# Activation halves one tile later, 64-bit conversion begun later, and tiles moved by 320 bytes in a one-core attention + MoE kernel

## The chip, the cores and the metric

The kernel runs on one core of one Trainium2 chip, as one launch. The metric is the device time of the launch in microseconds (us), the median of three runs. Engines are named as the profile names them: PE is TensorE, ACT is ScalarE, DVE is VectorE, POOL is GpSimd, SP issues DMAs. PEld is PE's weight load.

## The reference: what is computed

Three blocks follow one another.

1. Attention over q, k, v of 2 batches x 8 heads x 768 tokens x 64. Each row of q and k falls into one of 64 buckets by the signs of a projection; scores outside the own bucket are masked, then softmax and the product with v. The result, laid out as 1536 tokens x 512, is x.
2. A mixture of 4 experts, w1[e] 512 x 1024 and w2[e] 1024 x 512: the sum over e of p[:, e] * (relu(x @ w1[e]) @ w2[e]).
3. One dense layer pair on the result: h = x @ w_in (512 x 2048), g = 0 where h <= -1, h where h >= 1, (h + 1)^2 / 4 between, and the output is g @ w_out (2048 x 512). w_in and w_out arrive as 64-bit floats.

## The kernel before

**Units and jobs.** The hidden columns of blocks 2 and 3 are cut into 12 units u of 512: units 0 to 7 are the experts, 8 to 11 the dense pair. The tokens are cut into 12 tiles of 128. A *job* is one unit with a group of two or three token tiles; a job has four *tiles* f of 128 hidden columns. For each tile `l1b(j, f)` makes the first product on PE in a PSUM tile `mm` (12 matmuls of 384 columns, two buffers) and its activation on ACT, DVE and POOL; `l2b(j, f)` multiplies the activation of the job before with the second weight (9 matmuls of 512 columns into `o0`, `o1`, `o2`). Numbers are split into a high and a low half of 16 bits, so each activation leaves as `hh` and `hl`.

**First part (to about 445 us).** Attention and the first jobs, `JOBS_A`, are ordered together by the class `Order`, a list scheduler with costs and due times. The diff does not touch it.

**Second part, from the line `attx.close()`.** The order of the program is the order of the code. The main loop runs over jobs j and tiles f: `l1b(j + 1, f)`, a transposed token tile (`x_all`) if one is due, `step(j)`, `l2b(j, f)`, `step(j)`. Every engine executes its own instructions in this order. J0 is the first job of this part, JF = J0 + 2 the first with 16-bit weights. The units run 0, 2 to 6, 1 (two jobs each), then 7 and 8 to 11 (four jobs each).

**`step(j)`** fetches weights that are due (list `late`), moves one piece of x to 16 bits (`x_f16`, list `xq`, eight pieces), advances the bound of x for the dense pair (`x2_steps`), advances both weight generators (`w_steps`: the scan L1075 for the largest magnitude, `fin` for the scale, `conv_w` for the two 16-bit halves, L1194 to L1199) and advances `w64_steps` by one. `w64_steps` turns a 64-bit weight tile into f32: a load `r64`, one ACT instruction (`m64`, L1139), five on DVE (L1141 to L1150), and the scan on ACT (L1154 calls L1075); at most 16 finished tiles wait (`w64_ahead`).

**Riders.** `fin` needs a transpose and a small matmul on PE. They ride in the unused columns 384:512 of the next `mm` tile: `rider(ps)`, called right behind the tile's matmuls, issues the PE instruction and its small DVE instructions (`turn_over`, L1088 to L1095; `spread`, L1097 to L1101).

**The activation of units 8 to 11 (L1332 to L1337),** per tile: ACT reads `mm` twice (`ga`, `gg`), DVE squares `ga`, POOL adds it to `gg`, ACT scales the sum into `hh`, DVE makes `hl`:

```
act.activation(a[:, 0:n], ps[:, 0:n], AF.Relu, bias=half, scale=kh)
act.activation(gg[:, 0:n], ps[:, 0:n], AF.Relu, bias=nhalf, scale=kh)
dve.scalar_tensor_tensor(a[:, 0:n], a[:, 0:n], 1.0, a[:, 0:n], ALU.min, ALU.mult)
pool.tensor_tensor(gg[:, 0:n], gg[:, 0:n], a[:, 0:n], ALU.add)
act.activation(hh[:, 0:n], gg[:, 0:n], AF.Copy, scale=cc)
dve.scalar_tensor_tensor(hl[:, 0:n], gg[:, 0:n], cc, hh[:, 0:n], ALU.mult, ALU.subtract)
```

`mm` is free again when ACT has read it twice. `kh` and `cc` come from `k5` (`scales2`), made at a unit's first tile (for unit 8 at each job's first tile).

**Memory.** The tiles of pool `const` come first, then all others. `ident` is 512 bytes per partition, the others are small, rounded up to 32 bytes; they add up so that x0, acc, the weights and nearly all other large tiles begin 64 bytes past a multiple of 128 (192 past one of 256). The kv tiles xk0 to xk3, kb and vs are 3136, 3072 and 3072 bytes, 9280 together, so xk0 to xk3 stand at 192, 0, 64 and 128 past a multiple of 256.

Of the kernel before, what the change touches and what calls it, by code (L numbers as in the profile page):

```python
# [8 lines left out]
F32 = mybir.dt.float32  # L9
# [277 lines left out]
def attn_moe_kernel(ctx: ExitStack, tc, q, k, v, proj, probs, w1, w2, w_in, w_out, out):  # L287
# [668 lines left out]
    with tc.manual_schedule():  # L956
# [87 lines left out]
        r64 = ctx.enter_context(tc.tile_pool(name="r64", bufs=2))  # L1044
        s64 = ctx.enter_context(tc.tile_pool(name="s64", bufs=1))
        x16_p = ctx.enter_context(tc.tile_pool(name="x16", bufs=1))
        mode["h"] = h_p = ctx.enter_context(tc.tile_pool(name="hb", bufs=8))
        g_p = ctx.enter_context(tc.tile_pool(name="g", bufs=2))
        raw2_p = ctx.enter_context(tc.tile_pool(name="raw2", bufs=4))
        w64_ahead = 16  # L1050
        w64_p = ctx.enter_context(tc.tile_pool(name="w64", bufs=w64_ahead + 2))
# [3 lines left out]
        J0, J1 = len(JOBS_A), len(jobs)  # L1055
        JF = J0 + 2
        jobs_of = {u: [j for j, x in enumerate(jobs) if x[0] == u and j >= JF] for u in LB}
        late, pend, turn, x2q, xq = [], [], [], [], []
        seen, x_done = {1: set(), 2: set()}, []

        def mm_tile():
# [19 lines left out]
        def fin(am, n, e_out, s_out, age=2):  # L1081
            mx = t_p.tile([128, 1], F32, tag="mx", name="mx2")
            mt = t_p.tile([1, 1], F32, tag="mt", name="mt")
            dg = t_p.tile([1, 1], BF16, tag="dg", name="dg2")
            left = [2]
            dve.tensor_reduce(mx, am[:, 0:n], AX.X, ALU.max)

            def turn_over(ps):  # L1088
                pe.transpose(ps[0:1], mx, ident)
                dve.tensor_reduce(mt, ps[0:1], AX.X, ALU.max)  # L1090
                dve.tensor_scalar(mt, mt, 2.0 ** -100, 2.0 ** -14, ALU.max, ALU.mult)
                pow2(mt)
                dve.tensor_copy(dg, mt)
                left[0] -= 1
                soon(spread, age)  # L1095

            def spread(ps):  # L1097
                pe.matmul(ps[:, 0:1], ones[0:1], dg, start=True, stop=True)
                dve.tensor_copy(e_out, ps[:, 0:1])
                dve.reciprocal(s_out, ps[:, 0:1])  # L1100
                left[0] -= 1  # L1101

            soon(turn_over, age)
            while left[0]:
                yield "fin"
# [5 lines left out]
        def w64_steps():  # L1111
            order = []
            for u in range(8, 12):
                order += [(1, u, f) for f in range(4)] + [(2, u, f) for f in range(4)]
            rt = {}

            def fetch(i):
                if i >= len(order):
                    return
                kind, u, f = order[i]  # L1120
                s = 4 * u - 32 + f
                t = rt[i] = r64.tile([128, 512, 2], I32, tag="r64", name="r64")
                if kind == 1:
                    sp.dma_start(
                        t.rearrange("p (c f) t -> p c (f t)", c=KC),
                        w_in32[:, s * 256:s * 256 + 256].rearrange("(c p) f -> p c f", p=128),
                    )
                else:
                    sp.dma_start(t.rearrange("p f t -> p (f t)"), w_out32[s * 128:s * 128 + 128, :])

            for i in range(2):
                fetch(i)
            for i, key in enumerate(order):
                r = rt.pop(i)
# [12 lines left out]
                dve.scalar_tensor_tensor(m, r.bitcast(U16)[:, :, 1], 2.0 ** -36, m, ALU.mult, ALU.mult)  # L1147
                fetch(i + 2)
                yield
                dve.tensor_tensor(wv, t.bitcast(F32), m, ALU.add)  # L1150
                kind, u, f = key
                if f == 0:
                    am64[kind, u] = t_p.tile([128, 4], F32, tag="am64", name="am64", bufs=6)
                scan(wv, am64[kind, u][:, f:f + 1])  # L1154
                w64_t[key] = wv
                yield

        w64 = w64_steps()

# [43 lines left out]
        def w_steps(kind):  # L1203
            for n, u in enumerate(LB):
                if n == 0:
                    ew[kind, u], sw[kind, u] = ew_b[:, kind - 1:kind], sw_b[:, kind - 1:kind]
                else:
                    if u < 8:
                        am = t_p.tile([128, 4], F32, tag=f"am{kind}", name=f"am{kind}", bufs=2)
                        for f in range(4):  # L1210
                            while (kind, u, f) not in raw2:
                                yield False
                            scan(raw2[kind, u, f], am[:, f:f + 1])
                            yield
                    else:
                        while (kind, u, 3) not in w64_t:
                            yield "w64"
                        am = am64[kind, u]
                    ew[kind, u] = const.tile([128, 1], F32, name=f"ew{kind}_{u}")
                    sw[kind, u] = const.tile([128, 1], F32, name=f"sw{kind}_{u}")  # L1220
                    yield from fin(am, 4, ew[kind, u], sw[kind, u])
                for f in range(4):
                    while ((JF - 1 if n < 2 else jobs_of[LB[n - 2]][-1]), f) not in seen[kind]:
                        yield False
                    conv_w(kind, n, f)
                    yield

        wgen = {1: w_steps(1), 2: w_steps(2)}

        def need(kind, u, f):  # L1230
            while (kind, u, f) not in w16:
                got = next(wgen[kind])
                if got is False:
                    raise RuntimeError(f"weights {kind} {u} {f} too early")
                if got == "fin" and pend:
                    pend.pop(0)[1](mm_tile()[:, 384:512])
                if got == "w64":
                    next(w64)

# [54 lines left out]
        def grp(j):  # L1294
            return jobs[j][1][0] // 3

        def l1b(j, f):
            u, tts = jobs[j]
            n = 128 * len(tts)
# [3 lines left out]
            seen[1].add((j, f))  # L1303
            if j < JF:
                l1_mm(j, f, ps, range(KC))
                rider(ps)
                l1_hi(j, f, ps)
                l1_lo(j, f, ps)
                return
            b, c0 = tts[0] // 6, (tts[0] % 6) * 128  # L1310
            assert all(x_done.count(tt) == (tt >= 6) + (u >= 8) for tt in tts), (j, u, tts, f, x_done, J0, turn)
# [2 lines left out]
            for kc in range(KC):  # L1314
# [2 lines left out]
                pe.matmul(ps[:, 0:n], hi[:, ws], xh[:, kc, xs], start=(kc == 0), stop=False)  # L1317
                pe.matmul(ps[:, 0:n], hi[:, ws], xl[:, kc, xs], start=False, stop=False)  # L1318
                pe.matmul(ps[:, 0:n], lo[:, ws], xh[:, kc, xs], start=False, stop=(kc == KC - 1))  # L1319
            rider(ps)  # L1320
            hts[j, f] = hh, hl = [h_p.tile([128, 256], F32R, tag=f"h{y}", name=f"h{y}").bitcast(F16) for y in "hl"]
            gg = g_p.tile([128, 384], F32, tag="gg", name="gg")
            if u < 8:
                act.activation(gg[:, 0:n], ps[:, 0:n], AF.Relu, scale=2.0 ** -15)
                act.activation(hh[:, 0:n], gg[:, 0:n], AF.Copy)  # L1325
                dve.tensor_tensor(hl[:, 0:n], gg[:, 0:n], hh[:, 0:n], ALU.subtract)  # L1326
            else:
                if f == 0 and (u == 8 or grp(j) == 0):
                    scales2(u, slice(grp(j), grp(j) + 1) if u == 8 else slice(0, 4))
                k2, kh, gp, cc, ko = (k5[u][:, i, grp(j):grp(j) + 1] for i in range(5))  # L1330
# [2 lines left out]
                act.activation(gg[:, 0:n], ps[:, 0:n], AF.Relu, bias=nhalf, scale=kh)  # L1333
                dve.scalar_tensor_tensor(a[:, 0:n], a[:, 0:n], 1.0, a[:, 0:n], ALU.min, ALU.mult)  # L1334
                pool.tensor_tensor(gg[:, 0:n], gg[:, 0:n], a[:, 0:n], ALU.add)  # L1335
                act.activation(hh[:, 0:n], gg[:, 0:n], AF.Copy, scale=cc)  # L1336
                dve.scalar_tensor_tensor(hl[:, 0:n], gg[:, 0:n], cc, hh[:, 0:n], ALU.mult, ALU.subtract)  # L1337

        def l2b_mm(j, i, f, o):
            if j < JF:  # L1340
# [66 lines left out]
        def step(j):  # L1407
# [64 lines left out]
```

## Time and profile before

| | us |
|---|---|
| median of 3 runs (1083.91 to 1089.51) | 1084.42 |
| the profiled execution | 1092.18 |
| its span, first to last instruction | 1090.4 |
| PE busy | 980.6 (90%) |
| DVE, ACT, POOL busy | 708.9, 734.4, 347.8 |
| mean granted PE clock, share of full | 0.973 |

The profiled execution is 7.8 us above the median of the runs, and 1.8 us longer than its span. Busy shares are means over parts with different limits: attention and first jobs up to about 445 us; 16-bit expert jobs to about 765 us; the dense pair's 64 tiles from there to the end. Idle time in a row is the time before the instruction in which its engine did nothing, put down to what ended last. Matmuls are pipelined, so their durations overlap.

### The profile page before, as it was taken

Reading aid. Unit: us, or ns where it says so; the run is one execution under the profiler, and the core shown is the slowest. Engines: PE = TensorE matmul, PEld = TensorE weight load, DVE = VectorE, ACT = ScalarE, POOL = GpSimd, SP = SyncE. Lnnn points to the kernel's source line nnn. Section 1 sums busy time; section 2 is a strip of 40 time slices with the busy share of each in tenths; the row PEclk is TensorE's granted clock in tenths of the full one; section 3 lists DMA queues with packets and bytes.
Section 4 is the critical chain, followed back from the end, with each engine's and each line's share of the span. In section 5 each row is a group of like instructions: output and inputs, shape, how many; then the busy total and the mean of one; then the engine's idle time right before and its main releaser. Section 6 shows DMA issues by size and latency. Waiting matters only on the chain.

```text
span 1090.4 us, 19455 instructions
## 1 busy us (share of the span) xinstructions
PE 980.6 (90%) x6874; PEld 622.4 (57%) x6874; DVE 708.9 (65%) x1946; ACT 734.4 (67%) x1590; POOL 347.8 (32%) x382
## 2 busy tenths in 40 slices
PE   6668999999889999698999999999888878788998
PEld 2347777878778888564555555555444434344553
DVE  6799989898887873377766764446555445444434
ACT  6788888798887873276777766567655753645542
POOL 0323545444455544222111110032312431323221
PEclk9779999999999999999999999999989999999999
DMA  8899999999999794613443430001010111000002
GB/s 216 182 200 197 192 238 233 222 201 180 208 195 166 168 162 111 213 39 119 132 136 97 118 106 29 1 21 39 20 38 20 39 40 39 20 1 1 1 30 87
DMA packets 254835, 121.51 MB, mean 111 GB/s; under 512 B 180752, under 2 KB 239504, under 8 KB 254736
## 3 DMA queue, kind: packets, MB, share of 16 engines
q1 hardware_dynamic: 251904, 117.89, 48.3%
q10 hardware_dynamic: 2832, 2.36, 0.8%
q8 instruction: 54, 0.88, 0.4%
q14 instruction: 45, 0.37, 0.1%
HBM read 70.28 MB, written 3.15 MB: 67 GB/s over the span
## 4 chain that ended last, share of the span: by engine, by line
PE 41%; ACT 17%; DVE 17%; DMA 11%; issue 5%; POOL 5%; SPq 2%; POOLq 0%; ACTq 0%; DVEq 0%
DMA raw<-in_moe_w_dram 7%; POOL gg L1335 4%; PE o L1346 4%; PE mm L1317 4%; PE mm L1318 4%; PE mm L1319 4%; PE o L1348 4%; PE o L1347 4%; DVE ga L1334 3%; ACT hh L1336 3%; PE s L635 2%; ACT ga L1332 2%; ACT jw L1075 2%; PE m L867 2%; PE m L869 2%
## 5 line engine op out<-in xcount | busy, mean ns | idle before, releaser
L685 POOL TENSOR_TENSOR pn<-e,pn 128x192 f16<-128x192 f32 (+3 forms) x146 | 127.3, 876 | 192.2 <-DVE pn L685 55.1
L1335 POOL TENSOR_TENSOR gg<-gg,ga 128x384 f32<-128x384 f32 x64 | 63.7, 995 | 183.1 <-DVE ga L1334 183.1
L1337 DVE SCALAR_TENSOR_TENSOR hl<-gg,k,hh 128x384 f16<-128x384 f32 x64 | 39.6, 618 | 118.8 <-ACT hh L1336 118.8
L1336 ACT ACTIVATE hh<-gg,k 128x384 f16<-128x384 f32 x64 | 39.4, 615 | 98.3 <-POOL gg L1335 98.3
L657 DVE CUSTOM_DVE_ANT_0 e<-s,mk,sc 128x768 f32<-128x768 f32 x96 | 96.8, 1010 | 3.9 <-ACT acc L715 2.4
L1326 DVE TENSOR_TENSOR hl<-gg,hh 128x384 f16<-128x384 f32 x72 | 42.7, 593 | 82.8 <-ACT hh L1325 82.7
L849 PE MATMUL m<-x0h,w1h 128*128 128x256 f32 x304 | 91.7, 302 | 1.1 <-DVE acc L879 1.1
L635 PE MATMUL s<-xk,xq 128*128 128x384 f16 (+1 forms) x384 | 82.3, 340 | 9.8 <-DVE usm L657 8.1
L670 ACT ACTIVATE e<-e,usm 128x768 f32<-128x768 f32 x96 | 89.3, 930 | 2.5
L677 ACT ACTIVATE pn<-e 128x768 f16<-128x768 f32 (+3 forms) x118 | 84.4, 716 | 5.4 <-DMA pt<-pn 4.4
L850 PE MATMUL m<-x0l,w1h 128*128 128x256 f32 x304 | 85.9, 283 | 0.0
L851 PE MATMUL m<-x0h,w1l 128*128 128x256 f32 x304 | 85.9, 282 | 0.0
L1346 PE MATMUL o<-w2l,hh 128*128 128x512 f16 x216 | 82.2, 381 | 0.0
L1347 PE MATMUL o<-w2l,hh 128*128 128x512 f16 x216 | 82.1, 380 | 0.0
L1348 PE MATMUL o<-w2l,hl 128*128 128x512 f16 x216 | 81.9, 379 | 0.0
L1346 PE MATMUL o<-w2h,hh 128*128 128x512 f16 x192 | 73.6, 383 | 0.0
L1347 PE MATMUL o<-w2h,hh 128*128 128x512 f16 x192 | 73.4, 382 | 0.0
L1317 PE MATMUL mm<-x161h,w1l 128*128 128x384 f16 x192 | 63.4, 330 | 10.8 <-ACT gg L1333 7.7
L1348 PE MATMUL o<-w2h,hl 128*128 128x512 f16 x192 | 73.0, 380 | 0.0
L1317 PE MATMUL mm<-x161h,w1h 128*128 128x384 f16 x192 | 63.4, 330 | 6.2 <-ACT gg L1333 3.8
L1348 PEld LDWEIGHTS <-hl 128*128 128x128 f16 x408 | 40.1, 98 | 48.8 <-issue 1.1
L867 PE MATMUL m<-w2h,hh 128*128 128x512 f32 x152 | 64.6, 425 | 2.9 <-DVE hl L861 2.5
(258 smaller groups left out, 2913.1 us busy)
## 6 DMA issues: line engine op xcount, KB each, us to landing
raw<-in_moe_w_dram SPq DMA_DIRECT2D x127, 256.0 KB, 3.9
r<-in_moe_w_in_dram SPq DMA_DIRECT2D x16, 512.0 KB, 3.8
r<-in_moe_w_out_dram SPq DMA_DIRECT2D x16, 512.0 KB, 3.7
rawx<-in_moe_w_dram SPq DMA_DIRECT2D x24, 256.0 KB, 4.4
out_dram<-acc SPq DMA_DIRECT2D x12, 256.0 KB, 2.1
raw<-in_moe_w_dram ACTq DMA_DIRECT2D x9, 256.0 KB, 4.1
w<-in_moe_w_dram SPq DMA_DIRECT2D x8, 256.0 KB, 6.7
rk<-in_k_dram SPq DMA_DIRECT2D x5, 384.0 KB, 4.1
```

The lines of the kernel that those rows point to most:

```text
L635: pe.matmul(sps[:, j, 0:n], st["xq"][1 - i][:, hh * QG[pgs[m][0]][2] + c], st["x"][:, hh, 384 * j:384 * j + n], start=(i == 0), stop=(i == 1))
L657: dve.tensor_tensor_reduce(out=e.rearrange("p (a b) -> p a b", a=2), in0=u["s"][:, :, 0:384], in1=u["mk"].rearrange("p (a b) -> p a b", a= ...
L670: act.activation(u["e"], u["e"], AF.Exp, scale=-1.0, bias=sm[:, 2:3], accum_out=sm[:, 3:4])
L685: eng[e].tensor_tensor(u["pn"][:, 768 + c0:768 + c1], u["e"][:, c0:c1], u["pn"][:, c0:c1], ALU.subtract)
L849: pe.matmul(ps[:, 0:n], hi[:, ws], xh[:, kc, xs], start=(kc == 0), stop=False)
L850: pe.matmul(ps[:, 0:n], hi[:, ws], xl[:, kc, xs], start=False, stop=False)
L867: pe.matmul(o, hh[:, ts], whi, start=(f == 0), stop=False)
L1317: pe.matmul(ps[:, 0:n], hi[:, ws], xh[:, kc, xs], start=(kc == 0), stop=False)
L1335: pool.tensor_tensor(gg[:, 0:n], gg[:, 0:n], a[:, 0:n], ALU.add)
L1346: pe.matmul(o, hh[:, ts], whi, start=(f == 0), stop=False)
L1347: pe.matmul(o, hh[:, ts], wlo, start=False, stop=False)
L1348: pe.matmul(o, hl[:, ts], whi, start=False, stop=(f == 3))
```

## The change

The dense pair's `hh` and `hl` of a tile are kept as a function (`halves`) and issued one tile later, behind the next tile's `ga`, `gg`, squaring and POOL add (`split`); the last ones at the head of `l2b_last`. For this `gg`, `ga`, `tx` and `jw` have three buffers instead of two (`g`), and `hh`/`hl` seven instead of eight (`hb`). `rider` issues only PE's part and returns the DVE part (`rest`), called at the end of `l1b`. The scan of a converted 64-bit tile moves into the next call of `w64_steps`, together with the next tile's `m64`. `w64_step` is called only for j > JF, so the conversion begins 3 jobs later. `need(2, u)` makes sure that the second weight's scale is there. A `pad` of 320 bytes behind `ident` moves everything behind it.

```diff
     ident = const.tile([128, 128], F32, name="ident")
+    const.tile([128, 80], F32, name="pad")
...
-        mode["h"] = h_p = ctx.enter_context(tc.tile_pool(name="hb", bufs=8))
-        g_p = ctx.enter_context(tc.tile_pool(name="g", bufs=2))
+        mode["h"] = h_p = ctx.enter_context(tc.tile_pool(name="hb", bufs=7))
+        g_p = ctx.enter_context(tc.tile_pool(name="g", bufs=3))
...
             if pend and pend[0][0] <= 0:
-                pend.pop(0)[1](ps[:, 384:512])
+                return pend.pop(0)[1](ps[:, 384:512])
+            return lambda: None
...
             def turn_over(ps):
                 pe.transpose(ps[0:1], mx, ident)
-                dve.tensor_reduce(mt, ps[0:1], AX.X, ALU.max)
...
+                def rest():
+                    dve.tensor_reduce(mt, ps[0:1], AX.X, ALU.max)
...
+                return rest
...
                 if f == 0:
                     am64[kind, u] = t_p.tile([128, 4], F32, tag="am64", name="am64", bufs=6)
+                yield
                 scan(wv, am64[kind, u][:, f:f + 1])
                 w64_t[key] = wv
-                yield
...
-            rider(ps)
+            rest = rider(ps)
...
             else:
+                need(2, u)
...
                 pool.tensor_tensor(gg[:, 0:n], gg[:, 0:n], a[:, 0:n], ALU.add)
-                act.activation(hh[:, 0:n], gg[:, 0:n], AF.Copy, scale=cc)
-                dve.scalar_tensor_tensor(hl[:, 0:n], gg[:, 0:n], cc, hh[:, 0:n], ALU.mult, ALU.subtract)
+                split()
+
+                def halves():
+                    act.activation(hh[:, 0:n], gg[:, 0:n], AF.Copy, scale=cc)
+                    dve.scalar_tensor_tensor(hl[:, 0:n], gg[:, 0:n], cc, hh[:, 0:n], ALU.mult, ALU.subtract)
+
+                halve.append(halves)
+            rest()
...
         def l2b_last(j):
+            split()
...
-            w64_step()
+            if j > JF:
+                w64_step()
```

PE's and POOL's instructions keep their order from first to last; ACT, DVE and SP keep theirs up to the beginning of the second part.

ACT in unit 9, two tiles following one another, before (`w64` to `w2h` is a weight's conversion, `jw` a scan):

```order
L1332 ACTIVATE ga_12033<-mm_12017,half_104,k5_11942 128x384 [waits PE_49]
L1333 ACTIVATE gg_12032<-mm_12017,nhalf_105,k5_11942 128x384
L1336 ACTIVATE hh_12030<-gg_12032,k5_11942 128x384 [waits Pool_49]
L1197 ACTIVATE w64_11547<-w64_11547,sw2_10_11818 128x512
L1198 ACTIVATE w2h_12052<-w64_11547 128x512 [waits PE_49,Activation_49]
L1075 ACTIVATE jw_12057,am64_11923<-w64_11957 128x512 [waits DVE_49]
L1332 ACTIVATE ga_12075<-mm_12059,half_104,k5_11942 128x384 [waits PE_49]
L1333 ACTIVATE gg_12074<-mm_12059,nhalf_105,k5_11942 128x384
L1336 ACTIVATE hh_12072<-gg_12074,k5_11942 128x384 [waits Pool_49]
```

and the same two tiles now:

```order
L1350 ACTIVATE ga_12035<-mm_12019,half_105,k5_11945 128x384 [waits PE_49]
L1351 ACTIVATE gg_12034<-mm_12019,nhalf_106,k5_11945 128x384
L1357 ACTIVATE hh_11986<-gg_11988,k5_11945 128x384 [waits Pool_49]
L1208 ACTIVATE w64_11520<-w64_11520,sw2_10_11821 128x512
L1209 ACTIVATE w2h_12052<-w64_11520 128x512 [waits PE_49,Activation_49]
L1077 ACTIVATE jw_12056,am64_11910<-w64_11927 128x512 [waits DVE_49]
L1149 ACTIVATE m64_12058<-r64_11875 128x512 [waits DMAHW3_49]
L1350 ACTIVATE ga_12078<-mm_12062,half_105,k5_11945 128x384 [waits PE_49]
L1351 ACTIVATE gg_12077<-mm_12062,nhalf_106,k5_11945 128x384
L1357 ACTIVATE hh_12032<-gg_12034,k5_11945 128x384 [waits Pool_49]
```

Before, `hh` reads the `gg` that stands in the row above it; now it reads that of the tile before (`hh_12032` of `gg_12034` comes behind `gg_12077`), and `m64` has moved behind the scan.

SP at the beginning of the second part, before (`r64` are the 64-bit loads, `raw1` the first expert weight of the third unit):

```order
L1184 DMA w64_7702<-in_moe_w2_dram 128x512 [waits DMAHW0_49]
L1124 DMA r64_7792<-in_moe2_w_in_dram 128x4x256 [waits DMAHW1_49,Activation_49,Pool_49]
L1124 DMA r64_7794<-in_moe2_w_in_dram 128x4x256 [waits DMAHW2_49]
L1124 DMA r64_7872<-in_moe2_w_in_dram 128x4x256 [waits DMAHW1_49,DMAHW3_49,DVE_49,Activation_49]
L1124 DMA r64_8000<-in_moe2_w_in_dram 128x4x256 [waits DMAHW2_49,DMAHW4_49,DVE_49,Activation_49]
L1129 DMA r64_8127<-in_moe2_w_out_dram 128x1024 [waits DMAHW3_49,DMAHW5_49,DVE_49,Activation_49]
L1129 DMA r64_8284<-in_moe2_w_out_dram 128x1024 [waits DMAHW4_49,DMAHW6_49,DVE_49,Activation_49]
L1182 DMA raw1_8329<-in_moe_w1_dram 128x4x128 [waits DMAHW7_49]
```

and now, the last of four `raw1` loads, which follow the `w64` loads directly, and what comes behind it:

```order
L1193 DMA raw1_8279<-in_moe_w1_dram 128x4x128 [waits DMAHW4_49,DVE_49]
L1195 DMA raw2_8281<-in_moe_w2_dram 128x512 [waits DMAHW5_49,Pool_49]
L1195 DMA raw2_8283<-in_moe_w2_dram 128x512 [waits DMAHW6_49,Pool_49]
L1195 DMA raw2_8285<-in_moe_w2_dram 128x512 [waits DMAHW7_49,Pool_49]
L1195 DMA raw2_8287<-in_moe_w2_dram 128x512 [waits DMAHW0_49,Pool_49]
L1193 DMA rawx1_8289<-in_moe_w1_dram 128x4x128 [waits DMAHW1_49,PE_49,Pool_49]
L1193 DMA rawx1_8289<-in_moe_w1_dram 128x4x128 [waits DMAHW2_49]
L1193 DMA rawx1_8289<-in_moe_w1_dram 128x4x128 [waits DMAHW3_49]
L1193 DMA rawx1_8289<-in_moe_w1_dram 128x4x128 [waits DMAHW4_49]
L1134 DMA r64_8296<-in_moe2_w_in_dram 128x4x256 [waits DMAHW5_49]
L1134 DMA r64_8298<-in_moe2_w_in_dram 128x4x256 [waits DMAHW6_49]
```

The first `r64` loads have moved behind twelve weight loads of the third and fourth unit.

## Rows read from the trace of the kernel before

**Rows 1.** Busy time of each engine by stretches of the span (busy, instructions, granted clock).
```profile
60.00:420.00 360.00, 335.66 (x3443) 274.98 (x3443) 302.83 (x952) 291.90 (x699) 168.96 (x207) 0.99 1.00 195
450.00:480.00 30.00, 24.25 (x138) 19.21 (x138) 16.15 (x29) 15.54 (x33) 1.17 (x1) 0.89 0.39 117
540.00:720.00 180.00, 180.00 (x976) 94.01 (x974) 104.79 (x251) 123.14 (x269) 28.58 (x24) 1.00 0.25 74
764.50:858.60 94.10, 79.19 (x410) 41.13 (x408) 51.11 (x122) 56.59 (x106) 25.91 (x24) 0.95 0.10 29
858.60:945.20 86.60, 67.70 (x340) 33.89 (x339) 41.27 (x79) 48.48 (x88) 26.96 (x24) 0.96 0.13 37
945.20:1017.80 72.60, 63.04 (x329) 32.13 (x327) 33.84 (x66) 36.81 (x64) 21.55 (x21) 0.98 0.00 1
1017.80:1091.00 73.20, 67.34 (x356) 34.63 (x354) 31.48 (x56) 29.31 (x49) 16.07 (x17) 0.99 0.12 44
```

**Rows 2.** Who PE waited for from 764.5 to 1017.8 us (us, times, longest).
```profile
PE mm L1317 <- ACT gg L1333: 29.2, 17, 3.2
PE mm L1317 <- DVE ga L1334: 10.1, 5, 5.4
PE mm L1089 <- DVE mx L1086: 1.7, 2, 1.2
```

**Rows 3.** Groups of instructions by line over the span (busy, mean ns | idle before, releaser).
```profile
L1335 POOL TENSOR_TENSOR gg<-gg,ga 128x384 f32<-128x384 f32 x64 | 63.7, 995 | 183.1 <-DVE ga L1334 183.1
L1337 DVE SCALAR_TENSOR_TENSOR hl<-gg,k,hh 128x384 f16<-128x384 f32 x64 | 39.6, 618 | 118.8 <-ACT hh L1336 118.8
L1336 ACT ACTIVATE hh<-gg,k 128x384 f16<-128x384 f32 x64 | 39.4, 615 | 98.3 <-POOL gg L1335 98.3
```

**Rows 4.** One tile of unit 10 in order of time: ACT, DVE, POOL, ACT, DVE.
```profile
949.68 0.66 ACT L1333 ACTIVATE gg<-mm,nhalf,k 128x384 f32<-128x384 f32 x1
949.81 0.56 DVE L1334 SCALAR_TENSOR_TENSOR ga<-ga 128x384 f32<-128x384 f32 x1 [0.40 <-ACT ga L1332]
950.54 1.00 POOL L1335 TENSOR_TENSOR gg<-gg,ga 128x384 f32<-128x384 f32 x1 [2.33 <-DVE ga L1334]
951.57 0.61 ACT L1336 ACTIVATE hh<-gg,k 128x384 f16<-128x384 f32 x1 [1.23 <-POOL gg L1335]
952.22 0.62 DVE L1337 SCALAR_TENSOR_TENSOR hl<-gg,k,hh 128x384 f16<-128x384 f32 x1 [1.85 <-ACT hh L1336]
```

**Rows 5.** ACT's groups with the idle before them, unit 8, then unit 9.
```profile
L1332 ACT ACTIVATE ga<-mm,half,k 128x384 f32<-128x384 f32 x16 | 10.6, 664 | 8.8 <-DVE k L1290 3.5 <-DVE mt L1090 2.2 <-DVE s L1100 1.8
L1075 ACT ACTIVATE jw<-w 128x512 bf16<-128x512 f32 x5 | 3.1, 627 | 7.7 <-DVE w L1150 7.7
...
L1332 ACT ACTIVATE ga<-mm,half,k 128x384 f32<-128x384 f32 x16 | 10.5, 658 | 3.3 <-DVE mt L1090 1.9 <-DVE sw L1100 1.4
L1075 ACT ACTIVATE jw<-w 128x512 bf16<-128x512 f32 x6 | 3.8, 630 | 9.4 <-DVE w L1150 9.4
```

**Rows 6.** The beginning of the second part: waits of ACT and PE (440 to 540 us).
```profile
ACT m L1139 <- DMA r<-in_moe_w_in_dram: 7.3, 1, 7.3
PE mm L849 <- DVE hl L861: 8.2, 2, 5.2
PE mm L1317 <- ACT gg L1324: 2.8, 2, 2.5
```

**Rows 7.** Two conversions on POOL, and a DVE instruction beside the first.
```profile
844.53 0.69 DVE L1150 TENSOR_TENSOR w<-t,m 128x512 f32<-128x512 f32 x1
844.59 1.64 POOL L1199 TENSOR_TENSOR w1h<-w,w1h 128x512 f16<-128x512 f32 x1 [2.00 <-ACT w1h L1198]
850.29 1.16 POOL L1199 TENSOR_TENSOR w1h<-w,w1h 128x512 f16<-128x512 f32 x1 [2.00 <-ACT w1h L1198]
```

**Rows 8.** Tile xk: matmuls that read it (ns min/median/max) and its transposing DMAs.
```profile
L635 PE MATMUL s<-xk,xq x384: 324/328/533, 21.8 to 400.0; 128*128 128x390 f16 x96, 128*128 128x384 f16 x96
DMA to landing us min/median/max: 2.8/3.9/7.5
```

More of the change, by code (lines that the diff above doesn't have):

```diff
@@ L1057, in attn_moe_kernel @@
         jobs_of = {u: [j for j, x in enumerate(jobs) if x[0] == u and j >= JF] for u in LB}
-        late, pend, turn, x2q, xq = [], [], [], [], []
+        late, pend, turn, x2q, xq, halve = [], [], [], [], [], []
         seen, x_done = {1: set(), 2: set()}, []
@@ L1089, in turn_over, with rest @@
                 pe.transpose(ps[0:1], mx, ident)
-                dve.tensor_reduce(mt, ps[0:1], AX.X, ALU.max)
[L1091 to L1095, printed above, removed]
+                def rest():
+                    dve.tensor_reduce(mt, ps[0:1], AX.X, ALU.max)
+                    dve.tensor_scalar(mt, mt, 2.0 ** -100, 2.0 ** -14, ALU.max, ALU.mult)
+                    pow2(mt)
+                    dve.tensor_copy(dg, mt)
+                    left[0] -= 1
+                    soon(spread, age)
+                return rest
             def spread(ps):
                 pe.matmul(ps[:, 0:1], ones[0:1], dg, start=True, stop=True)
-                dve.tensor_copy(e_out, ps[:, 0:1])
-                dve.reciprocal(s_out, ps[:, 0:1])
-                left[0] -= 1
+                def rest():
+                    dve.tensor_copy(e_out, ps[:, 0:1])
+                    dve.reciprocal(s_out, ps[:, 0:1])
+                    left[0] -= 1
+                return rest
             soon(turn_over, age)
@@ L1164, in attn_moe_kernel @@
         w16, ew, sw, raw2, rawx = {}, {}, {}, {}, {}
+        scaled = set()
         def fetch_w(kind, n, f):
@@ L1221, in w_steps @@
                     yield from fin(am, 4, ew[kind, u], sw[kind, u])
+                scaled.add((kind, u))
                 for f in range(4):
@@ L1228, in attn_moe_kernel, with need @@
         wgen = {1: w_steps(1), 2: w_steps(2)}
-        def need(kind, u, f):
-            while (kind, u, f) not in w16:
+        def need(kind, u, f=None):
+            while (kind, u) not in scaled if f is None else (kind, u, f) not in w16:
                 got = next(wgen[kind])
@@ L1235, in need @@
                 if got == "fin" and pend:
-                    pend.pop(0)[1](mm_tile()[:, 384:512])
+                    pend.pop(0)[1](mm_tile()[:, 384:512])()
                 if got == "w64":
@@ L1295, in grp, with split @@
             return jobs[j][1][0] // 3
+        def split():
+            while halve:
+                halve.pop(0)()
         def l1b(j, f):
@@ L1319, in l1b @@
                 pe.matmul(ps[:, 0:n], lo[:, ws], xh[:, kc, xs], start=False, stop=(kc == KC - 1))
-            rider(ps)
+            rest = rider(ps)
             hts[j, f] = hh, hl = [h_p.tile([128, 256], F32R, tag=f"h{y}", name=f"h{y}").bitcast(F16) for y in "hl"]
@@ L1335, in l1b @@
                 pool.tensor_tensor(gg[:, 0:n], gg[:, 0:n], a[:, 0:n], ALU.add)
-                act.activation(hh[:, 0:n], gg[:, 0:n], AF.Copy, scale=cc)
-                dve.scalar_tensor_tensor(hl[:, 0:n], gg[:, 0:n], cc, hh[:, 0:n], ALU.mult, ALU.subtract)
+                split()
[3 more added lines that the diff above has]
+                halve.append(halves)
+            rest()
         def l2b_mm(j, i, f, o):
```

## The prediction

> **What bounds the kernel now.** I read the busy time by stretches first. From 60 to 420 us (attention) PE, DVE and ACT are busy 336, 303 and 292 of 360 us and the mean DMA share is 1.00: several limits at once, and none that a reordering behind 445 us can touch [rows 1]. From 540 to 720 us PE is busy all of the time at full clock (2.4 GHz), with 976 matmuls, 0.184 us each: here PE is the bound, and work taken off ACT or DVE gives nothing. In the dense pair's part PE is idle again: three stretches of 16 tiles, units 8, 9 and 10, last 94.1, 86.6 and 72.6 us with PE busy 79.2, 67.7 and 63.0 [rows 1]. The last unit is close to PE's pace.
>
> Then the waits of PE in those three stretches: 39.3 us of them (29.2 + 10.1) are for an `mm` tile whose two readers on ACT are late [rows 2] (where the row names DVE's `ga`, DVE holds up the buffer that ACT writes). So ACT is late, but it isn't busy: 56.6, 48.5 and 36.8 us [rows 1]. The groups by line say why: ahead of `hh` ACT stands 98.3 us over 64 tiles, 1.54 each, for POOL, and POOL waits for DVE's square [rows 3]. One tile in order of time shows the ring: `gg` is through at 950.34, DVE's square at 950.37, POOL adds for 1.00, and ACT begins `hh` at 951.57 after 1.23 us of nothing; DVE then stands 1.85 for `hh` [rows 4]. ACT's next `ga`, which would free PE's tile, is queued behind that `hh`.
>
> **The change part by part.**
>
> *Halves one tile later.* Now ACT's `hh` belongs to a sum that POOL made a tile ago. One pace of PE is 21 x 0.184 = 3.9 us, POOL's part is done about 1.2 us behind `gg`, so the 1.54 us per tile go. What PE can get back: its 39.3 us of waits [rows 2], and the clock that it lost while waiting: the mean granted clock is 0.95, 0.96 and 0.98 there, which is 0.05 x 94.1 + 0.04 x 86.6 + 0.02 x 72.6 = 9.6 us. Together 49. A second count: 410, 340 and 329 matmuls at 0.184 would need 75.6, 62.7 and 60.7 us, 199 instead of 253.3, a gain of 54 [rows 1]; some records may be missing, so I take 49 and 54 as an upper end.
>
> Is ACT then fast enough? Its busy time and the idle that stays (the waits for `k5` and riders, and the scan behind DVE's add) come to 56.6 + 8.8 + 7.7 = 73.1 us for unit 8 and 48.5 + 3.3 + 9.4 = 61.2 for unit 9 [rows 1, 5], against PE's 75.6 and 62.7. It fits, but with 0.1 us per tile to spare, if none of those waits shrink. They should: the riders' small DVE work now stands behind the halves, and the scan comes a call later. What is late next is DVE. It is busy 51.1 and 41.3 us, 3.2 and 2.6 per tile. Its `hl` now waits for `hh` of the tile before, which on ACT stands behind `gg`: the square (0.56) runs beside `gg` (0.66), then 0.61 of `hh` pass, so some 0.7 us of standing are left of the 1.85 [rows 4]. That gives 3.9 and 3.3 per tile, under PE's 4.7 and 3.9.
>
> New is that `hl` runs beside POOL's add, which before always stood between. A POOL conversion beside DVE's two-input add took 1.64 instead of 1.16 us [rows 7], so the price is about 0.5 us for one of the two per tile. On POOL it is covered: 995 ns of 3.9. On DVE it gives 4.4 and 3.8 per tile; for unit 9 that is PE's own pace. The Trainium skill (SBUF — State Buffer, "Who interferes with whom") speaks against the change here: a DVE instruction with two SBUF inputs and a reading GpSimd instruction share a port, and the later one is blocked completely. By that rule `hl` could not begin before POOL's add ends, some 0.3 us later than I count, and DVE would be at 3.6 in unit 9, still inside PE's pace.
>
> For all that I take off 4 us (0.25 us in each of 16 tiles): 49 - 4 = **45**. Lower end 21 (rival 1), upper 54. The smaller buffer count of `hh`/`hl` (7) costs nothing: the slot of tile t was read by PE with tile t - 7, three paces before the write. `need(2, u)` issues nothing new at that place.
>
> *64-bit conversion three jobs later.* Early in the second part ACT's first `m64` stands 7.3 us for its load, which SP issues behind 16 weight loads, and with it the relu that frees PE's tile: 5.2 us of PE's waits are this one [rows 6]. Now no `m64` stands there. The stretch around it has a clock of 0.89 [rows 1], 0.11 x 30 = 3.3 us at most, partly from the other 3.0 us wait of that row (8.2 - 5.2), which stays. I count 5.2 + 1 = **6**, between 3 and 9. The wait isn't only removed: the first `r64` load is now queued on SP behind twelve weight loads, of which the last four can't start before POOL has read x0, and `m64` follows a few instructions behind the last of these pieces. I expect ACT to stand there for 2 to 4 us, as it does now at about the same place (PE: 2.5 us of L1317 [rows 6]); one goes, one comes, 0. In return SP is no longer held by `r64` buffers there. The conversion itself moves into a stretch where PE is full and ACT is busy 123 of 180 us [rows 1]; its 16 tiles ahead need 96 calls, 12 jobs, and stand ready 5 jobs before unit 8.
>
> *Tiles moved by 320 bytes.* Before, nearly all large tiles share one offset, so the trace shows no other for them. What it has are xk0 to xk3 at four offsets: 384 matmuls on them differ by 1% between shortest and median (324 and 328 ns) [rows 8]. I take 0. Both signs stay open for the DMAs, whose share is 1.00 from 60 to 420 us: at most 3.6 us per per cent of transfer time [rows 1].
>
> **Sum.** 45 + 6 + 0 = 51. The profiled execution would go from 1092.2 to 1041, the median, 7.8 lower, from 1084.4 to **1033 us**. Its own range is 1024 (54 + 6) to 1045 (35 + 4).
>
> **Rivals.**
> 1. *A new wait takes the old one's place* (chance 0.14). ACT's margin in units 8 and 9 is 0.1 us per tile and DVE's in unit 9 about as small. If DVE stands 1.3 instead of 0.7 us before `hl`, or ACT keeps 0.5 us per tile that I let go, the 48 tiles lose 0.5 each, 24 us: **1057**. For it: the small margins. Against it: the waits that remain in ACT's rows are upper values.
> 2. *Transfers become faster by the new offsets* (0.08). 5% of 360 us: 18 us more, **1015**. For it: the DMA share of 1.00. Against it: three engines are nearly full there too, and the four xk tiles. The Trainium skill (DMA: Bandwidth & Descriptors, "How a descriptor splits into AXI transactions") says that a piece not starting at a multiple of 256 bytes fetches more than it uses; for the first weights' 512 bytes at 192 that is, an estimate from its table, 22 beats instead of 16, by which those loads alone would shrink by a quarter. No run here shows it yet.
> 3. *Transfers become slower by the new offsets* (0.03), the other side. Same place, same 3.6 us per per cent; it decides from 16% on (57 us), where the median would stand at 1090. For it: only that no row shows the large tiles at the new offset. Against it: xk0 to xk3.
> 4. *The change does not do what it says* (0.03): PE's tile is freed late for another reason, such as the wait for DVE's `k5`, and `hh` was only the last in a row. Then **1080 to 1085**. Against it: 98.3 us in one wait, and a ring that closes in every tile [rows 3, 4].
>
> **How the numbers follow.** The forecast has 0.72. A measurement of this kernel can tell about 0.5%, 5.4 us, from no change. Faster by more: 0.72 + 0.14 + 0.08 = 0.94; within it 0.03; slower 0.03. The range runs from rival 2's 1015 to rival 1's 1057 and leaves out some 0.15.
>
> **What would show it.** In the changed profile: idle before `hh` near 0 instead of 98.3, and before `hl` about 45 (0.7 x 64) instead of 118.8; POOL's add longer than 995 ns; PE's waits for `gg` and `ga` under 8 us; the three stretches at about 77, 65 and 63 us with a clock of 1.00; no 7.3 us wait of the first `m64`, but one of 2 to 4 three jobs later; the part up to 440 us unchanged to 1%. Wrong would be: a like amount of idle in front of `ga` or the scan on ACT (rival 1), or attention ending earlier or later by over 4 us (rivals 2, 3).

## The result, and the profile after

| | before | after |
|---|---|---|
| median, us | 1086.97 (1083.91 to 1091.04, 4 runs) | 1019.97 (1019.86 to 1020.15, 4 runs) |
| ratio, 95% interval | | 0.9382 [0.9344, 0.942] |
| profiled execution, its span | 1092.18, 1090.4 | 1019.93, 1018.1 |

The change gives 67 us; 51 were forecast. Line numbers behind L308 are moved: `ga` is now L1350, `gg` L1351, the square L1352, POOL's add L1353, `hh` L1357, `hl` L1358.

From the page of the kernel after: busy time, and the chain that ended last by engine.

```profile
PE 963.4 (95%) x6874; PEld 619.1 (61%) x6874; DVE 731.4 (72%) x1946; ACT 732.2 (72%) x1590; POOL 353.8 (35%) x382
PE 62%; DVE 14%; ACT 10%; DMA 9%; issue 4%; SPq 1%; POOL 1%; DVEq 0%; ACTq 0%; POOLq 0%
```

PE holds 62% of the chain, where it held 41%. DVE is busy 22.5 us longer than before (708.9) with as many instructions. The groups by line say why: `hl` takes 58.4 instead of 39.6 us, 18.8 of the 22.5. The first two are to be held against [rows 3].

```profile
L1353 POOL TENSOR_TENSOR gg<-gg,ga 128x384 f32<-128x384 f32 x64 | 71.0, 1109 | 153.0 <-DVE ga L1352 142.6
L1358 DVE SCALAR_TENSOR_TENSOR hl<-gg,k,hh 128x384 f16<-128x384 f32 x64 | 58.4, 913 | 20.3 <-ACT hh L1357 20.0
L1350 ACT ACTIVATE ga<-mm,half,k 128x384 f32<-128x384 f32 x64 | 42.7, 667 | 67.9 <-PE mm L1336 46.7 <-DVE k L1302 12.8 <-PE mm L1091 4.4
L1357 ACT ACTIVATE hh<-gg,k 128x384 f16<-128x384 f32 x64 | 39.0, 610 | 2.5 <-POOL gg L1353 2.4
```

Idle time before `hh` has gone from 98.3 to 2.5 us. ACT now stands before `ga`, and for PE: it is ahead. `hl` costs 0.3 us more apiece, POOL's add 0.11 more.

Who PE waited for in units 8 to 10 (746 to 948 us) of the kernel after; before, the rows for `gg` and `ga` held 39.3 us [rows 2]:

```profile
PE mm L1334 <- DVE mt L1094: 3.7, 3, 2.6
PE mm L1334 <- DVE sw L1108: 1.6, 1, 1.6
PE mm L1334 <- ACT gg L1351: 1.2, 2, 0.6
PE mm L1091 <- DVE mx L1088: 0.6, 1, 0.6
```

The stretches from one unit's first POOL add to the next one's, units 8, 9 and 10, kernel after (us; busy PE, PEld, DVE, ACT, POOL; granted clock, DMA share, GB/s):

```profile
745.92:822.35 76.43, 69.87 (x387) 37.58 (x387) 56.06 (x117) 58.22 (x112) 27.80 (x25) 1.00 0.12 40
822.35:888.14 65.79, 65.24 (x352) 34.04 (x350) 49.65 (x82) 45.19 (x83) 29.27 (x24) 1.00 0.14 41
888.14:947.75 59.61, 59.61 (x324) 31.46 (x323) 37.65 (x64) 34.31 (x62) 23.21 (x20) 1.00 0.00 1
```

Unit 10 is at PE's pace throughout, unit 9 nearly; unit 8 has 6.6 us of idle PE left, with the waits for the riders' `mt` and `sw`. The granted clock is at its upper level, 2.4 GHz, in all three.

So far it is as forecast. But the dense part accounts for 48 us only. Three instants cut each profiled execution: the first `mm` tile of the second part, POOL's first add of the dense part, and its last.

| kernel (label of its run) | median us | ratio to before, 95% | first `mm` at | to first add | first to last add |
|---|---|---|---|---|---|
| before | 1086.91 to 1089.77 | 1 | 440.2 | 329.7 | 307.3 |
| after | 1019.97 | 0.9382 [0.9344, 0.942] | 430.7 | 315.2 | 258.9 |
| e1_pad: before + pad | 1078.63 | 0.9902 [0.9873, 0.9931] | 434.6 | 325.3 | 306.9 |
| e3_pad256: before + pad of 256 bytes | 1089.56 | 1.0006 [0.9986, 1.0025] | 442.0 | 327.1 | 306.9 |
| e4_pad128: before + pad of 192 bytes | 1087.46 | 0.9994 [0.9971, 1.0017] | 440.7 | 327.9 | 306.9 |
| e5_late64_only: before + later conversion | 1077.14 | 0.9897 [0.9869, 0.9926] | 436.6 | 319.4 | 306.9 |
| e2_nopad: after, no pad | 1028.54 | 0.945 [0.9418, 0.9482] | 442.0 | 315.6 | 260.5 |
| e6_early64: after, conversion early | 1029.55 | 0.9453 [0.943, 0.9476] | 431.8 | 323.9 | 259.1 |
| e7_at_once: after, halves in place | 1065.82 | 0.9794 [0.9761, 0.9827] | 430.3 | 316.8 | 311.8 |
| e8_riders: after, riders in place | 1024.84 | 0.9412 [0.9383, 0.9441] | 433.7 | 314.0 | 265.5 |
| e12_scan: after, scan in place | 1033.35 | 0.9498 [0.9468, 0.9529] | 428.6 | 322.5 | 267.1 |
| e11_g2: after, buffer counts of before | 1021.04 | 0.9387 [0.9363, 0.941] | 428.9 | 313.8 | 258.7 |
| e9_between: riders before `hl` | 1013.93 | 0.933 [0.9301, 0.936] | 430.4 | 315.5 | 255.8 |
| e10_first: halves first in the tile | 1011.24 | 0.9302 [0.9278, 0.9326] | 428.4 | 315.0 | 252.4 |

Between the two profiled executions the second part begins 9.5 us earlier, its way to the first add is 14.5 us shorter, and the dense part 48.4: that is 72.4, of which 24 lie outside the dense part, where 6 were forecast. The instants are those of one execution each, which can lie some us off its median (e7_at_once 7.0, e2_nopad 4.7 and e8_riders 3.5 above, e11_g2 4.5 below). Prices below are differences of the ratios times 1087 us, since each ratio was measured against the kernel before on the same chip; the intervals leave each price uncertain by some 3 to 5 us.

### The profile page after: what moved, and what is told of

It reads as the page before. It is cut to its first block, busy times and chain, and to the rows that moved or that the text cites. A ratio compares the mean times of both kernels' runs of the same rounds, so it can differ in the third digit from the quotient of the medians.

```text
span 1018.1 us, 19428 instructions
## 1 busy us (share of the span) xinstructions
PE 963.4 (95%) x6874; PEld 619.1 (61%) x6874; DVE 731.4 (72%) x1946; ACT 732.2 (72%) x1590; POOL 353.8 (35%) x382
## 4 chain that ended last, share of the span: by engine, by line
PE 62%; DVE 14%; ACT 10%; DMA 9%; issue 4%; SPq 1%; POOL 1%; DVEq 0%; ACTq 0%; POOLq 0%
PE mm L1334 7%; PE mm L1335 7%; PE mm L1336 7%; PE o L1370 6%; PE o L1372 6%; PE o L1371 6%; DMA raw<-in_moe_w_dram 5%; PE s L636 3%; DVE hl L1358 2%; PE m L868 2%; PE m L850 2%; PE m L870 2%; PE m L851 2%; PE m L869 2%; PE m L852 2%
## 5 line engine op out<-in xcount | busy, mean ns | idle before, releaser
L1353 POOL TENSOR_TENSOR gg<-gg,ga 128x384 f32<-128x384 f32 x64 | 71.0, 1109 | 153.0 <-DVE ga L1352 142.6
L1350 ACT ACTIVATE ga<-mm,half,k 128x384 f32<-128x384 f32 x64 | 42.7, 667 | 67.9 <-PE mm L1336 46.7
L1352 DVE SCALAR_TENSOR_TENSOR ga<-ga 128x384 f32<-128x384 f32 x64 | 38.4, 601 | 63.8 <-ACT ga L1350 63.8
L1358 DVE SCALAR_TENSOR_TENSOR hl<-gg,k,hh 128x384 f16<-128x384 f32 x64 | 58.4, 913 | 20.3 <-ACT hh L1357 20.0
L1341 ACT ACTIVATE gg<-mm 128x384 f32<-128x384 f32 x72 | 34.8, 483 | 45.1 <-PE mm L1104 20.9
```

## Experiments

**The pad.** Four kernels. e1_pad and e2_nopad put the pad in alone and take it out alone:

```
     ident = const.tile([128, 128], F32, name="ident")
+    const.tile([128, 80], F32, name="pad")
```

> The kernel before with the 320-byte pad alone: its large tiles start at 0 instead of 192 modulo 256 bytes, and no instruction moves. Theory A (the offset makes the transfers shorter): in the changed kernel the DMA engines needed 516 instead of 540 us for the same packets and attention ended 9.5 us earlier, so here too: 8 to 12 us faster than before (about 0.991), first `mm` tile of the second part at about 431 us. Theory B (the 9.5 us are chance or come from elsewhere): no change, within 3 us, first tile at about 440.

> The changed kernel without the pad: all its other parts at the old offset of 192 modulo 256. Theory A: about 10 us slower than the changed kernel, 1030 us, first `mm` tile at about 440. Theory B: 1020 us, as the changed kernel.

e3_pad256 and e4_pad128 have `[128, 64]` and `[128, 48]` there, in the kernel before.

> Control: the kernel before with a pad of 256 bytes. Every tile moves, but the large ones stay at 192 modulo 256. Theory A: the time of before, within 3 us, first `mm` tile at about 440, and packets as long as before (540 us for each DMA engine). If any move of the tiles shifts the time (theory B'), it differs from before by as much as the 320-byte pad does, with either sign.

> The kernel before with a pad of 192 bytes: the large tiles start at 128 modulo 256, a multiple of 128 bytes and not of 256. If multiples of 128 are enough: as the 320-byte pad, 8 to 12 us faster than before. If it takes multiples of 256: between the two, 0 to 6 us faster than before.

The pad alone takes 1.0% off (10.7 us); without it the changed kernel is 7.4 us slower, with intervals that just overlap. Both agree with theory A. The control, which moves every tile and leaves the large ones at 192 modulo 256, does nothing, so it isn't the move. At 128 modulo 256 nothing is gained either (0.9994): a multiple of 128 bytes is not enough here, and the one pad that ends at a multiple of 256 is enough. Whether every multiple of 256 is, no run shows. The queue's rows of the pages (packets, MB, share of 16 engines), before, e1_pad, e4_pad128:

```profile
span 1090.4 us, 19455 instructions
...
q1 hardware_dynamic: 251904, 117.89, 48.3%
```

```profile
span 1079.3 us, 19455 instructions
...
q1 hardware_dynamic: 251904, 117.89, 46.9%
```

```profile
span 1088.8 us, 19455 instructions
...
q1 hardware_dynamic: 251904, 117.89, 47.7%
```

Share times span: the same packets take 526.7 us before, 506.2 with the pad (3.9% less), 519.4 at 128 (the 540 of the expectations is all four queues, 49.6%). What that is worth to ACT in the first part is seen in its waits for weight loads, before (60 to 440 us) and e1_pad (60 to 434):

```profile
ACT w2h L831 <- DMA raw<-in_moe_w_dram: 15.8, 14, 2.3
ACT w1h L831 <- DMA raw<-in_moe_w_dram: 9.6, 8, 2.5
```

```profile
ACT w2h L832 <- DMA raw<-in_moe_w_dram: 12.4, 11, 2.4
ACT w1h L832 <- DMA raw<-in_moe_w_dram: 5.8, 8, 1.7
```

25.4 against 18.2 us. The control shows 21.6 and e4_pad128 24.2 there, so single executions differ by some of that; the ratios are what decides. Over all fourteen kernels the column of the first `mm` tile falls into two groups: 436.6 to 442.0 (mean 440.3) in the five whose large tiles stand at 192 or 128 modulo 256, 428.4 to 434.6 (mean 430.8) in the nine at 0. So nearly all of the gain lies in the first part, 9.5 us.

The trace has each packet's size and time, and they say where the gain is. Of the 20 us that the packets of e1_pad take less (summed, over 16 engines), 17.3 are those of 256 bytes, all of them in the first part (273.0 to 255.7), and 3.4 those of 512 (77.8 to 74.4). The median packet is the same in both kernels: 18 ns for 256 bytes, 27 for 512. What changes is how many are slow: the packets over 1.1 times the median are 13.5% before, 12.6% at 128 and 3.8% with the pad for 256 bytes, and 18.0, 13.2 and 2.1% for 512. The Trainium skill (DMA: Bandwidth & Descriptors, "How a descriptor splits into AXI transactions") has each transaction start at a multiple of 256 bytes; e4_pad128 agrees that 128 does not do. But the unchanged median shows that most packets cost the same at either offset; why some become slow stays open.

**The conversion's start.** e5_late64_only is the kernel before with this, e6_early64 the changed kernel without it:

```
-            w64_step()
+            if j > JF:
+                w64_step()
```

> The kernel before with the 64-bit conversion begun three jobs later and nothing else. Without the pad the changed kernel took 1028.5 us, 59.6 less than before; of these 46.8 lie between the first and the last add of POOL in the dense part, and 14 between the first `mm` tile and that first add (315.5 us instead of 329.7). Theory A: the later conversion makes all of the 14 (the 7.3 us wait of ACT, what follows of it on DVE, and the clock of 0.91 and 0.94): that stretch 316 us, in all 14 faster (0.987). Theory B: it makes the 6 that were forecast, and the riders and the scans the rest: 324 us, 6 faster (0.9945).

> The changed kernel with the 64-bit conversion begun at once, as before. Theory A: the 14 us come back, 1034 us, the first `mm` tile to the first add 329 us. Theory B: 1026 us and 321; and if the halves need the room that the later start leaves on ACT, the dense part grows too.

Alone it takes 1.03% off (11.2 us), nearer to theory A's 14 than to B's 6; undone in the changed kernel it costs 7.7 us, nearer to B's. So it makes some 8 to 11 of the 14; the scan, undone further down, is the next part. The way to the first add goes from 329.7 to 319.4 and from 315.2 to 323.9. What PE got back is seen in three stretches from the first `mm` tile on, before and e5_late64_only:

```profile
440.20:480.00 39.80, 31.03 (x190) 25.79 (x191) 20.19 (x46) 18.11 (x39) 5.43 (x8) 0.91 0.52 159
480.00:510.00 30.00, 29.31 (x158) 15.81 (x157) 24.53 (x43) 20.44 (x44) 14.26 (x11) 1.00 0.14 39
510.00:540.00 30.00, 27.55 (x144) 14.14 (x143) 19.31 (x48) 24.06 (x53) 5.08 (x4) 0.94 0.68 208
```

```profile
436.60:476.40 39.80, 36.26 (x224) 29.51 (x225) 18.14 (x44) 21.28 (x44) 7.77 (x10) 0.96 0.55 165
476.40:506.40 30.00, 29.28 (x159) 15.21 (x158) 19.59 (x38) 18.56 (x42) 10.71 (x9) 1.00 0.28 81
506.40:536.40 30.00, 29.84 (x161) 15.44 (x160) 20.29 (x48) 23.96 (x54) 5.08 (x4) 1.00 0.39 122
```

PE is busy 7.5 us more of the 99.8 (95.4 against 87.9), and the clock of 0.91 and 0.94 becomes 0.96 and 1.00: 0.05 x 39.8 + 0.06 x 30 = 3.8 us. 11.3 together, an estimate, against the 10.3 by which the way got shorter.

**The halves' place.** e7_at_once is the changed kernel with:

```
-                split()
-
                 def halves():
...
-                halve.append(halves)
+                halves()
```

> The changed kernel with each tile's halves at once behind POOL's add, and all else as changed. Theory A (the halves' place is what the dense part gained by): 45 us come back, 1065 us, first to last add 305 us, about 98 us of idle time before `hh`, and DVE's `hl` at 0.62 instead of 0.91 us. Rival: riders behind the tile's work, the third `gg` buffer and the later scans do half of it by themselves: about 1043 us.

44.8 us come back (0.9794 against 0.9382); the rival's 1043 is out. What is left is what pad and later start give by themselves (0.9902 x 0.9897 = 0.980): without the halves' move, those of riders and scan together gain nothing. The groups of e7_at_once are those of before:

```profile
L1353 POOL TENSOR_TENSOR gg<-gg,ga 128x384 f32<-128x384 f32 x64 | 63.7, 995 | 187.0 <-DVE ga L1352 181.6
L1356 DVE SCALAR_TENSOR_TENSOR hl<-gg,k,hh 128x384 f16<-128x384 f32 x64 | 39.6, 618 | 118.1 <-ACT hh L1355 116.3
L1355 ACT ACTIVATE hh<-gg,k 128x384 f16<-128x384 f32 x64 | 39.3, 615 | 106.7 <-POOL gg L1353 106.7
```

The idle time before `hh` is back, and `hl` and the add have their old durations. Who PE waited for in units 8 to 10 of it (746 to 960 us):

```profile
PE mm L1334 <- ACT gg L1351: 16.0, 8, 3.5
PE mm L1334 <- DVE mt L1094: 13.2, 5, 4.2
PE mm L1334 <- DVE sw L1108: 7.3, 4, 2.7
```

More than half of it is now put down to the riders' `mt` and `sw`, which stand behind a late `hl` here. So the 44.8 us are the price of the halves' place with riders and scan in their new ones; no run moves the halves alone.

**Riders, scan, buffers.** Three more parts undone in the changed kernel. e8_riders calls `rider(ps)()` behind the tile's matmuls and drops both `rest()`. e12_scan:

```
-                yield
                 scan(wv, am64[kind, u][:, f:f + 1])
                 w64_t[key] = wv
+                yield
```

e11_g2 has `bufs=8` for `hb` and `bufs=2` for `g`.

> The changed kernel with the riders' work on DVE where it stood, ahead of the tile's own, and all else as changed. Theory A (riders matter little as long as ACT is ahead of PE): within 3 us of the changed kernel, 1020 to 1023; the waits of PE for `mt` and `sw` (5.5 us) go and some for `gg` and `ga` come. Theory B (they make 8 us of the early gain): 1028 us.

> The changed kernel with the scan of a converted 64-bit tile where it stood: right behind DVE's add of that tile instead of a call later. Theory A (the scan's place matters, since ACT has little room in unit 8 and stands behind the scan for DVE's `w`): the idle time of ACT before `jw` goes from 30.3 back towards 53 us, and PE waits for `ga` and `gg` in unit 8: 3 to 6 us slower than the changed kernel, 1023 to 1026. Theory B (ACT is ahead of PE with the halves where they are now, so its waits are its own): 1019 to 1022.

> The changed kernel with the buffer counts of before: 2 for `gg` and 8 for the halves instead of 3 and 7. `gg` of a tile then waits for `hl` of the tile two before, which comes behind POOL's add of the tile between. Theory A: that `hl` is done about 2 us ahead of it at PE's pace of 3.9: no change, 1019 to 1022. Theory B (the third buffer is what lets the halves wait): ACT stands for `hl` ahead of `gg`, some 0.3 us a tile, 1030 to 1040.

The buffers do nothing (0.9387): with two of them `gg` is free in time but for 3.6 us of ACT's waits in the dense part. The riders give 3.3 us, with intervals that overlap, so it isn't clear of noise. In the trace, of an execution 3.5 us above its median, the dense part is 6.6 us longer without their move; PE's waits for `mt` and `sw` are gone there, and 5.9 us for `gg` and 3.7 for `ga` have come, as theory A said. None of this was in theory B's early part (314.0). The scan was the surprise: in its old place it costs 12.6 us, more than either theory had, 7.3 of the trace's on the way to the first add (3.5 of them one wait of PE for a rider's `mx`) and 8.2 in the dense part. ACT's group in unit 8, after (745.92 to 822.35) and e12_scan (751 to 831):

```profile
L1077 ACT ACTIVATE jw<-w 128x512 bf16<-128x512 f32 x6 | 3.8, 627 | 5.5 <-DVE w L1160 5.5
```

```profile
L1077 ACT ACTIVATE jw<-w 128x512 bf16<-128x512 f32 x6 | 3.8, 627 | 12.5 <-DVE w L1160 12.5
```

PE's waits for `gg` in e12_scan (748 to 960 us) are back with it:

```profile
PE mm L1334 <- ACT gg L1351: 5.6, 4, 1.8
PE mm L1334 <- DVE mt L1094: 5.2, 3, 3.4
PE mm L1334 <- DVE sw L1108: 1.3, 1, 1.3
```

Taken out one at a time, pad, start, halves, riders and scan cost 7.4 + 7.7 + 44.8 + 3.3 + 12.6 = 75.8 us, more than the 67 of all. That fits e7_at_once, by which riders and scan gain only with the halves. But all five differences use the same 0.9382, uncertain by 4 us in each, so the excess is not clear of noise.

**Two other places.** The riders' work still held PE in unit 8. e9_between puts it between the tile's square and the halves of the tile before:

```
                 dve.tensor_tensor(hl[:, 0:n], gg[:, 0:n], hh[:, 0:n], ALU.subtract)
+                rest()
             else:
...
                 pool.tensor_tensor(gg[:, 0:n], gg[:, 0:n], a[:, 0:n], ALU.add)
+                rest()
                 split()
...
                 halve.append(halves)
-            rest()
```

The first `rest()` is for the expert units, where it stays at the tile's end.

> The changed kernel with the riders' work on DVE between the tile's square and the halves of the tile before (now: behind the halves). Theory A: in the changed profile DVE stands about 0.5 us ahead of `hl` for `hh`, and PE waits 5.3 us in unit 8 for `mt` and `sw`, which stand behind `hl` and still hold the `mm` tile; between the two they cost nothing and free the tile earlier: 4 to 5 us faster than the changed kernel, 1015 to 1016, and the waits for `mt` and `sw` gone. Theory B: any work of riders ahead of `hl` delays the next square as it did when they stood in front of the tile (1024.8): 1020 to 1025.

e10_first instead begins each tile with the halves of the tile before:

```
                 k2, kh, gp, cc, ko = (k5[u][:, i, grp(j):grp(j) + 1] for i in range(5))
+                split()
...
                 pool.tensor_tensor(gg[:, 0:n], gg[:, 0:n], a[:, 0:n], ALU.add)
-                split()
```

> The changed kernel with the halves of the tile before ahead of the tile's `ga` instead of behind POOL's add; DVE's `hl` then runs beside ACT's `ga` and `gg`, and POOL's add has DVE free of two-input work. Theory A (the longer `hl` and add come from running side by side, the later of the two held until the earlier is nearly through): `hl` back at 0.62 us instead of 0.91 and the add at 1.00 instead of 1.11. Rival: they are longer for another reason (the place of the buffers, PE at full clock): 0.91 and 1.11 as now. For the time: ACT frees PE's tile 0.6 us later in each tile; PE's pace has room for that except in unit 8: 1020 to 1026.

Both are faster than the changed kernel, by 5.7 and 8.7 us; only for e10_first do the intervals stand apart (0.9302 [0.9278, 0.9326] against 0.9382 [0.9344, 0.942]). In e9_between PE's waits for `mt` and `sw` in units 8 to 10 are down from 5.3 to 1.7 us:

```profile
PE mm L1334 <- ACT gg L1352: 1.8, 2, 1.2
PE mm L1334 <- DVE mt L1094: 1.5, 1, 1.5
PE mm L1091 <- DVE mx L1088: 0.6, 1, 0.6
PE mm L1334 <- DVE sw L1108: 0.2, 1, 0.2
```

The time of e10_first was forecast as 1020 to 1026, and this was wrong: freeing PE's tile 0.6 us later shows no cost, PE's waits for `mt` and `sw` in the dense part are down to 0.2 us, and DVE is busy 16 us less (715.4 against 731.4). Its groups:

```profile
L1354 POOL TENSOR_TENSOR gg<-gg,ga 128x384 f32<-128x384 f32 x64 | 67.5, 1054 | 157.4 <-DVE ga L1353 144.9
L1358 DVE SCALAR_TENSOR_TENSOR hl<-gg,k,hh 128x384 f16<-128x384 f32 x64 | 43.9, 686 | 67.0 <-ACT hh L1357 65.6
```

No `hl` runs beside an add of POOL there, and 56 of the 64 take 0.60 to 0.62 us. The mean of 0.69 comes from the 8 others, 1.11 to 1.30 us, each of which begins while POOL converts a weight (L1210). The add, 1.05, meets other two-input work of DVE: beside the add of L1160 it takes 1.29. That speaks for theory A, and so do the pairs further down.

## Why the prediction was right, and where it was wrong

The measured 1020 lies below the forecast's own 1024 to 1045 (which took 35 and 4 as lower ends where the working has 21 and 3), and inside the stated 1015 to 1057 only because that went down to rival 2's time. The largest term was right; two small ones, 6 and 0, were both too low, by some 8 us each.

*Halves, 45.* Right in its ring and in its size: undone, 44.8 us come back, with riders and scan left in their new places; the three stretches last 76.4, 65.8 and 59.6 us (77, 65 and 63 forecast), idle time before `hh` is 2.5 and PE's waits for `gg` 1.2. Two steps in it were loose. The margin of ACT, 0.1 us per tile, was said to hold because the scan's and the riders' waits would shrink, and they were given no price. At least the scan is what makes it hold: in its old place the kernel is 12.6 us slower, 8.2 of the trace's in the dense part. For the riders, 3.3 us, it is not clear of noise. Rival 1's wait, ACT standing behind something else, was thus real, and the scan's move took it away. And DVE's margin was counted with 0.7 us of standing before `hl`, 45 in all; it is 20.3, and `hl` itself has become 18.8 longer.

*Port, -4.* The side by side of `hl` and POOL's add came, at 0.3 us per tile on DVE and 0.11 on POOL, within the 0.5 taken for one of them. PE is at or near its pace in units 9 and 10 all the same, so that most of it is covered; e10_first, which avoids it, is 8.7 us faster, but has the riders earlier too, so how much of that is the port's stays open.

*Conversion, 6.* The failed step is the size of this term. The way to the first add is 14.1 us shorter without the pad (329.7 to 315.6), where 6 stood, outside the 3 to 9. Three things were mispriced. The step "one goes, one comes, 0": the new wait of `m64` came, as long as said or a little longer,

```profile
ACT m L1149 <- DMA r<-in_moe_w_in_dram: 4.3, 1, 4.3
```

(ACT's waits, 430 to 746 us, after), but no wait of PE follows from it. PE's waits on that way are these three, where the list of before adds up to 14.9 us, most of it in [rows 6]. The wait for `hl`, 8.2, is 2.5 now, about the 5.2 less of the forecast; another 5.7 us went beside it:

```profile
PE mm L850 <- DVE hl L862: 2.5, 1, 2.5
PE mm L850 <- DVE acc L880: 0.8, 1, 0.8
PE mm L1334 <- DVE sw L1108: 0.2, 1, 0.2
```

The clock was given 1 us; in e5_late64_only it is 3.8. And the scan, 7.3 us of this stretch when undone, was no term at all.

*Offset, 0.* The second failed step is to take 0 because matmuls on the four xk tiles differ by 1%. Those rows are matmuls; they say nothing of transfers, whose price was named (3.6 us per per cent) and then not taken. Rival 2, with a chance of 0.08, had the right mechanism, and its sign came: attention ends 9.5 us earlier, where over 4 was to be the sign. It is 10.7 us alone and 7.4 on top of the rest, not 18: the packets' time falls by 3.9%, the first part's by 2.2% (440.3 to 430.8, the means of the two groups); three engines are nearly full there too. The estimate from the Trainium skill's page named above, a quarter less for the 512-byte loads, is not seen: the time of the 512-byte packets falls by 4.4% (77.8 to 74.4), and their median of 27 ns not at all.

So 45 + 6 + 0 became about 45 + 14 + 8: the 67 of the medians. The profiled executions differ by 72, as the one before was 5 to 8 us above its medians. Rivals 3 and 4 are out: e1_pad is faster, and PE's waits went with those before `hh`.

## What to carry to other kernels

When a chain through a slow engine returns to the engine that frees the bound engine's buffer, issue the chain's last part one tile later, and put it where its two-input work does not meet the slow engine's: first in the next tile beat last here by 8.7 us, though how much of that is the meeting stays open. Give a price to every small instruction that changes its place in an in-order queue; a scan moved by one call was worth more here than the wait that was looked for. Where transfers are dense, try large tiles at a multiple of 256 bytes: here it gave 1.0%, and 128 modulo 256 gave nothing.

## What the runs showed of the hardware

How DVE and POOL share is sharper than a mean shows. Two tiles of unit 9, kernel after, DVE and POOL in order of time:

```profile
869.33 0.99 POOL L1353 TENSOR_TENSOR gg<-gg,ga 128x384 f32<-128x384 f32 x1 [3.19 <-DVE ga L1352]
869.67 1.07 DVE L1358 SCALAR_TENSOR_TENSOR hl<-gg,k,hh 128x384 f16<-128x384 f32 x1 [0.51 <-ACT hh L1357]
...
872.19 0.61 DVE L1358 SCALAR_TENSOR_TENSOR hl<-gg,k,hh 128x384 f16<-128x384 f32 x1
872.44 1.22 POOL L1353 TENSOR_TENSOR gg<-gg,ga 128x384 f32<-128x384 f32 x1 [2.12 <-DVE ga L1352]
```

Whichever starts first keeps its own time; the other is held. Of the 64 tiles POOL starts first in 40, and `hl`, however far behind it begins (0.03 to 0.36 us), ends 1.41 us after the add began: 0.80 and its own 0.61. In 23 `hl` is first, by 0.08 to 0.25 us, keeps 0.60 to 0.62, and the add ends about 1.47 us after `hl` began (in two tiles 2.07). The Trainium skill (SBUF — State Buffer, "Who interferes with whom") says that the later one is blocked while the first runs; the trace agrees that the later one is held, but not to the end of the first: the add lets go at 0.80 of its 0.99 us, and by the same count `hl` at about 0.48 of its 0.61 (1.47 less the add's own 0.99).
